# A transformer block on one Trainium2 core: six of seven down-projection pairs turned into products of 512 columns, and GELU in one activation

## The chip, the core and the metric

The kernel runs on one core of one Trainium2 chip. The metric is the device time of one execution in microseconds; where several runs are given, their median counts. The core has five engines with a queue each, which run side by side and meet at semaphores: TensorE (PE: matrix products into PSUM), VectorE (DVE), ScalarE (ACT), GpSimd (POOL) and SyncE (SP), which here issues nearly all DMAs.

## What is computed

One block on x [2048, 512]: attention with 32 query and 8 key/value heads over the last 512 cached keys, then a gated feed-forward layer with 1792 inner columns. Shifts, scales and gates come from a conditioning vector.

```python
h = _layernorm(x) * (1 + ca) + sa
x = x + ga * attention(h, k_cache, v_cache, wq, wo)
h = _layernorm(x) * (1 + cb) + sb
x = x + gb * ((gelu(h @ w_gate) * (h @ w_up)) @ w_down)     # gelu: tanh form
```

Inputs and outputs are float32.

## The kernel before

**Number format.** PE works in float16. Each float32 operand is split into a high and a low half (`halves`, `split_post`, the two lines in `result`), and one product is three matmuls, low-high, high-high and high-low (`mm3`, line 85, whose matmuls all carry line 89). Scales per weight tile keep the halves in range (`f_spread`, `d_spread`); column tables such as `fsc`, `finv`, `dsc`, `dysc` hold them and their inverses.

**Stages.** The rows are worked in two halves of 1024, each as two blocks of 512 (`qb`) of four tiles of 128. Attention is a list of 128 units (row half, head pair, block, head) in four steps each, T = 512 steps in all; its order is written out by hand, step by step, inside `tc.manual_schedule`: entries under `at(t, ...)` run at step t, and DMA loads get due times from `sched` and spare positions from `spare`. In the second half of these steps the feed-forward weights are prepared too: `prep_set` for gate and up weights and `prep_wd` for down weights load them, scale and split them on POOL, and store the halves in HBM (`store`), from where `fetch` brings them back later.

**The feed-forward stage** comes after the hand-ordered part. There only the SP queue keeps the written order; for the other engines a planner puts the instructions in order at build time, by priority (the order in which the program lists them) and by when its model says that inputs and buffers are ready. On the chip each queue then runs in that fixed order. The inner dimension has 14 tiles, taken as 7 pairs (NP); per row half and pair n there is a set of products for gate (m = 0) and one for up (m = 1), so q counts 28 of them (NQ), q = 2n + m. Each set is a 2 x 2 block product by seven block products instead of eight (a Strassen-Winograd form): `PROD` names their operands, `CHAIN` the PSUM bank (a, b or c) into which each is accumulated, `ORDER` = (1, 2, 6, 7, 5, 4, 3) their order. Bank a is read by ACT between products 1, 6, 7 and 4 of its chain (`keep`), and the next product of the chain must wait for that copy. One block product is two groups of three matmuls with 512 columns. `result` takes each finished block "11", "21", "12" or "22" (inner tile, row block): for gate it applies GELU in four instructions (ACT square, DVE, ACT tanh, DVE), for up it multiplies the two and splits the outcome into the halves `at`, A[n, key].

**Down-projection.** `y_tasks` makes for one row tile of 128 and one pair two times three matmuls: the `at` slice is the stationary operand, the prepared weights (`wo`, fetched from `kept`) are the moving one with 512 output columns. The result lies with rows on partitions, and DVE adds it, scaled by a column `dysc`, to the running row tile `acc` (line 942). That is 8 tasks of 6 matmuls a pair and row half. The loop at the end of `block_kernel` puts such tasks (`nexty`) between the products: at positions 1, 2, 5 and 6 of the seven, `y_next` takes one. `tick` counts positions for things put off by `put_off`. When the last pair of a row half is added, `f_final` stores the row tile to the output and later loads the next half's tile `y1` (attention's result, stored to HBM by `attn_final`) into the freed buffer. There are 8 `acc` buffers.

**Turning by DMA** is in the kernel already: the softmax rows `p` and the normalised rows of the second half (`ln_turned`, `xh` to `xt`) are turned by `dma_start_transpose` on two-byte elements, issued by SP.

**PSUM.** Eight banks: 5 under the tag "acc" (also for b and c of the sets and for `py`), 2 under "s", 1 under "qa".

Of the kernel before, what the change touches and what calls it, by code (L numbers as in the profile page):

```python
# [9 lines left out]

F32 = mybir.dt.float32
F16 = mybir.dt.float16
BF16 = mybir.dt.bfloat16
AF = mybir.ActivationFunctionType
ALU = mybir.AluOpType
AX = mybir.AxisListType

P = 128
# [20 lines left out]
GU = 2.0 ** -38  # L39
PRE = 2.0 ** -20  # L40
TINY = 1e-36
NOT = 10
LDGAP = 1
NRAW = 5
NRW = 2
GW = 3
NACC = 5
NP16 = 4
# [7 lines left out]
SETPOS = (20, 14, 13, 12, 10, 8)  # L56
SETPOS2 = (18, 12, 11, 10, 9, 7)
TAIL = 12
GELU_A = 0.044715
GELU_C = 0.7978845608028654  # L60


@with_exitstack
def block_kernel(ctx: ExitStack, tc: tile.TileContext, x, kT, v, wq, wo, wg, wu, wd, cT, wc, wm, out):
# [105 lines left out]
        ST[name] = const.tile([P, n], F32, name=name)  # L170

    for name, n in (("kmax", HKV), ("kinv", HKV), ("vmax", HKV), ("vsc", HKV), ("wsc", HQ // 2), ("qsc", HQ // 2),
                    ("ksc", HQ // 2), ("osc", HKV), ("ysc", HKV), ("fsc", NF), ("finv", NF), ("tsc", NF),
                    ("dsc", NF // 2), ("dysc", NF // 2), ("ma", 1), ("mf", 1), ("gam", 2)):
        stats(name, n)

    def col(name, i=0):
        return ST[name][:, i:i + 1]
# [99 lines left out]
    def o_spread(qd, m, more):  # L278
# [10 lines left out]

        then(second)  # L290

    def f_spread(i, m):
        w = little("lw", 1, 2)
        norm2(w, m, 2, 1.0 / TOP13)
        pool_ts(col("finv", i), w, col("mf"))
        pool_ts(col("tsc", i), col("finv", i), GELU_A * GELU_C)
        then(lambda: nc.vector.reciprocal(col("fsc", i), w))

    def d_spread(n, m, more):
        w, t = little("lw", 1, 2), little("lt", 1, 2)  # L300
        norm2(w, m, 2, 1.0)
        pool_ts(w, w, col("gam", 1), 1.0 / TOP14)
        pool_ts(w, w, 1e-30, 1.0, ALU.max)
        pool_ts(t, col("finv", 2 * n), 2.0 ** 19, col("finv", 2 * n + 1))
        pool_ts(col("dysc", n), t, 2.0 ** 19, w)

        def second():
            nc.vector.reciprocal(col("dsc", n), w)
            more()

        then(second)
# [636 lines left out]
    def attn_final(ti):  # L948
        y1[ti] = dram.tile([P, D], F32, name=f"y{ti}")
        dma(y1[ti], acc[ti])  # L950
        nxt = (ti + 2 * QT) % NT
        if ti < 2 * QT:
            own, steps = ln_tile(2, ti, lambda: acc[ti])
            own()
            for d, fn in zip((1, 5, 8, 9, 10, 12, 13), steps):
                at(("w", now[0] + d), fn)
            at(now[0] + 12, lambda: load_acc(nxt, rows_of(x, nxt)))
        else:
            ln_last(ti - 2 * QT)
            at(now[0] + 3, lambda: load_acc(nxt, y1[nxt]))  # L960

    def scores(t):
        u, i = divmod(t, 4)
# [291 lines left out]
    def f_items(q, hold=None):  # L1255
        n, m = divmod(q, 2)
        st = {}
        done = set()

        def add(k, src):  # L1260
            nc.vector.tensor_tensor(st[k], st[k], st[src], op=ALU.add)

        def gelu(key, src):
            b = {}

            def square():
                b["sq"] = pool.tile([P, QB], F32, tag="k", name="sq", bufs=2)
                nc.scalar.activation(b["sq"], src, AF.Square, scale=col("finv", f_scale(q)))

            def inner():  # L1270
                nc.vector.scalar_tensor_tensor(b["sq"], b["sq"], 1.0 / GELU_A, src, op0=ALU.add, op1=ALU.mult)

            def tanh():
                nc.scalar.activation(b["sq"], b["sq"], AF.Tanh, scale=col("tsc", f_scale(q)))

            def outer():
                dst = tmp("fg") if key == "21" else src
                nc.vector.scalar_tensor_tensor(dst, b["sq"], 1.0, src, op0=ALU.add, op1=ALU.mult)
                G[n, key] = dst

            return square, inner, tanh, outer

        def result(key, src):
            if m == 0:
                for step in gelu(key, src):
                    step()
            else:
                g = G.pop((n, key))
                nc.vector.scalar_tensor_tensor(g, g, 0.5 * GU, src, op0=ALU.mult, op1=ALU.mult)  # L1289
                t = pair("ot", "at", NOT)  # L1290
                nc.scalar.activation(t[:, 0, :], g, AF.Copy)  # L1291
                nc.vector.tensor_tensor(t[:, 1, :], g, t[:, 0, :], op=ALU.subtract)
                A[n, key] = t

        def out_(key, src):
            if not hold:
                result(key, src)
            else:
                hold.append(gelu(key, src))

        def place(k):
            if m == 0:
                return tmp("fg")
# [72 lines left out]

    def prep_wd(n, b):
        m, st = {}, {}
        outs = [staged() for _ in range(2)]

        def load(k):
            st[k] = raw("raw")
            dma(st[k], wd[(2 * n + k) * P:(2 * n + k + 1) * P, :])

        def stat(k):
            if not m:
                m["m"] = little("lm", 4, dtype=BF16)
            sumsq(m["m"][:, k:k + 1], st[k])

        def more():  # L1390
            m["g"] = pool.tile([P, D], F32, tag="gs", name="gs", bufs=1)
            pool_ts(m["g"], rows[5], col("dsc", n))
# [8 lines left out]
        sched(b, (lambda: load(0), [lambda: stat(0), nop]), b + 7)  # L1401
        sched(b + 1, (lambda: load(1), [lambda: stat(1), spread, nop]), b + 4, b + 9)
        for k in range(2):
            sched(b + 7 + 2 * k, (outs[k][1], [lambda k=k: make(k), lambda k=k: store(("wd", n, k), outs[k][0]["t"], 0)]), b + 10 + 2 * k)

    at(T // 2 + 34, lambda: mod_row(5))
    for n in range(NP):
# [1 line left out]
        prep_set(2 * n, b)  # L1409
        prep_set(2 * n + 1, b + 13)  # L1410
        prep_wd(n, b + 21)
    for k in range(2):
        at(T - 1 + 2 * k, lambda k=k: WO.update({("f", 0, k): fetch(("wd", 0, k), get_wo())}))
# [4 lines left out]
    pending = {"raw": [], "rw": []}  # L1418
    loads.sort(key=lambda l: l[0])
    released = {"raw": [0] * NRAW, "rw": [0] * NRW}  # L1420
    for pos, (load, steps), kind, ahead in loads:
        assert len(pos) == len(steps), (pos, len(steps))
        go = pos[0] - ahead
# [140 lines left out]
        at(("f", q, k), *fns)  # L1564

    for n in range(1, 2 * NP):
        for k in range(2):
            f_at(2 * n + 1, 2 * k, lambda n=n, k=k: WO.update({("f", n, k): fetch(("wd", n % NP, k), get_wo())}))
    for q in range(3, NQ):
        for k, at_ in ((0, 2), (3, 2), (1, 3), (2, 4)):  # L1570
            f_at(q - 1, at_, lambda q=q, k=k: set_fetch(("f", q), ("f", q % (2 * NP)), k))
# [18 lines left out]
                step(q + 2 * off, fn)  # L1590

    def f_final(ti):
        if ti >= 2 * QT:
            dma(rows_of(out, ti), acc[ti])
        else:
            put_off(2, lambda: dma(rows_of(out, ti), acc[ti]))
            put_off(5, lambda: load_acc(ti + 2 * QT, y1[ti + 2 * QT]))

    f_done = {(0, k) for k in ORDER} | {(1, 1), (1, 2), (1, 6)}
    for q in range(NQ):  # L1600
        n, m = divmod(q, 2)
        its = items(NG + q) if q < 2 else f_items(q)
        for k, pk in enumerate(ORDER):
            if (q, pk) not in f_done:
                all_of(its[pk])
            run(("f", q, k))
            tick()
            if k in ((1, 2, 5, 6) if q < NQ - 1 else (1, 5)):
                y_next()
        if m == 1:  # L1610
            for qi, (a, b) in enumerate((("11", "21"), ("12", "22"))):
                for i in range(QT):
                    nexty.append(y_tasks((2 * (n // NP) + qi) * QT + i, [lambda n=n, a=a: A[n, a], lambda n=n, b=b: A[n, b]],
                                         [("f", n, 0), ("f", n, 1)], col("dysc", n % NP), f_final if n % NP == NP - 1 else None))
    while nexty:
        y_next()
    while waits_:
        tick()
    assert not later, list(later)
# [34 lines left out]
```

## Time and profile before

| | |
|---|---|
| three timed runs | 1749.55, 1749.55, 1749.95 us; median 1749.55 |
| span of the profiled execution | 1746.6 us, its own time; the median of the runs is 2.95 us more |
| matmuls of the down-projection | 672 |
| clock granted to PE | full in every slice |

The profile is one execution. The span runs from the first to the last instruction; what lies around it (the 2.95 us) is not in the trace. Busy time of an engine counts its instructions, without waits. In a group row the engine, the operation, the tile written and the tiles read stand first, then the shapes, the count, busy us and mean ns; behind the second bar stands the idle time of the engine ahead of these instructions and what ended it. Timeline rows begin with the start and the length in us.

### The profile page before, as it was taken

The numbers are of one execution on the slowest core, as the hardware profiler recorded it, in microseconds if no ns is written. First come the engines' busy times: TensorE is split into PE (matmuls) and PEld (weight loads), VectorE is DVE, ScalarE is ACT, GpSimd is POOL, SyncE is SP. The second block draws the span as 40 slices with busy tenths as digits, with TensorE's granted clock in tenths as the row PEclk, the third lists the DMA queues.
The fourth block names the chain that finished last, engine by engine and source line by source line (L and its number), as shares of the span: only waits on it lengthen the run. The fifth ranks groups of instructions, "written<-read, shape, count | busy, mean of one in ns | idle before, by whom it ended". The sixth has DMA issues, their size and how long they took to land.

```text
span 1746.6 us, 25966 instructions
## 1 busy us (share of the span) xinstructions
PE 1724.3 (99%) x8080; PEld 792.8 (45%) x8082; DVE 1449.5 (83%) x2509; ACT 1248.3 (71%) x2806; POOL 906.2 (52%) x1127
## 2 busy tenths in 40 slices
PE   7999999999999999999999999999999999999999
PEld 5444444444444444444444444444444444444443
DVE  7898898888889999888888888888886788667676
ACT  6988788888879777888777777878774555334342
POOL 4889778776788884655474565555521224000000
PEclk9999999999999999999999999999999999999999
DMA  7999999999999998999999999999985763252222
GB/s 235 219 206 212 209 217 206 223 208 221 212 218 232 207 211 182 212 211 234 208 197 218 203 219 202 210 214 216 193 181 137 207 185 99 83 178 87 88 76 76
DMA packets 667499, 329.72 MB, mean 189 GB/s; under 512 B 561504, under 2 KB 580192, under 8 KB 667360
## 3 DMA queue, kind: packets, MB, share of 16 engines
q1 hardware_dynamic: 667072, 327.54, 81.9%
q8 instruction: 64, 1.05, 0.3%
q14 instruction: 75, 0.61, 0.1%
q10 hardware_dynamic: 288, 0.52, 0.1%
HBM read 131.73 MB, written 59.90 MB: 110 GB/s over the span
## 4 chain that ended last, share of the span: by engine, by line
PE 85%; DVE 4%; ACT 4%; issue 3%; DMA 2%; POOL 1%; SPq 0%; POOLq 0%; ACTq 0%; DVEq 0%
PE py L89 24%; PE ps L89 17%; PE po L89 17%; PE qa L89 8%; PE fa L89 6%; PE qc L89 4%; PE fc L89 3%; PE qb L89 2%; PE fb L89 1%; ACT ee L982 1%; PE pq L89 1%; ACT p L994 1%; DVE nm L973 1%; DMA cb<-hs 1%; POOL xh L534 1%
## 5 line engine op out<-in xcount | busy, mean ns | idle before, releaser
L982 ACT ACTIVATE ee<-ps,nm 128x512 f32<-128x512 f32 x512 | 350.2, 684 | 199.7 <-DVE nm L973 196.4
L999 DVE SCALAR_TENSOR_TENSOR p<-ee,rr,p 128x512 f16<-128x512 f32 x512 | 458.6, 896 | 4.1 <-ACT p L994 3.6
L973 DVE TENSOR_REDUCE nm<-ps 128x1 f32<-128x512 f32 x512 | 350.4, 684 | 113.0 <-PE ps L89 109.9
L89 PE MATMUL ps<-k,qt 128*128 128x512 f16 x1536 | 414.9, 379 | 5.4 <-ACT ee L982 4.4
L89 PE MATMUL po<-pt,v 128*128 128x512 f16 x1536 | 373.0, 379 | 1.6 <-DMA pt<-p 1.6
L994 ACT ACTIVATE p<-ee,rr 128x512 f16<-128x512 f32 x512 | 364.4, 712 | 12.4 <-DVE rr L990 9.0
L89 PE MATMUL py<-wo,ot 128*128 128x512 f16 x1536 | 371.5, 379 | 0.0
L89 PEld LDWEIGHTS <-w 128*128 128x128 f16 x2184 | 213.5, 98 | 259.8 <-issue 2.0
L89 PEld LDWEIGHTS <-v 128*128 128x128 f16 x1536 | 149.9, 98 | 183.7 <-DMA pt<-p 2.3
L89 PEld LDWEIGHTS <-ot 128*128 128x128 f16 x1536 | 150.2, 98 | 181.7 <-DVE ot L730 0.5
L89 PEld LDWEIGHTS <-qt 128*128 128x128 f16 x1536 | 145.9, 98 | 176.6 <-issue 4.0
L89 PE MATMUL py<-wo,at 128*128 128x512 f16 x672 | 161.6, 379 | 0.3 <-ACT at L1291 0.3
L730 DVE SCALAR_TENSOR_TENSOR ot<-po,ot 128x512 f16<-128x512 f32 x128 | 87.8, 686 | 30.0 <-ACT ot L729 29.3
L89 PEld LDWEIGHTS <-at 128*128 128x128 f16 x672 | 65.6, 98 | 80.0 <-ACT at L1291 0.7
L942 DVE SCALAR_TENSOR_TENSOR acc<-py,dysc,acc 128x512 f32<-128x512 f32 x112 | 81.2, 746 | 23.4 <-PE py L89 20.6
L982 ACT ACTIVATION_READ_ACCUMULATOR ee<-ps,nm 128x1 f32 x512 | 99.9, 195 | 0.0
L942 DVE SCALAR_TENSOR_TENSOR acc<-py,ysc,acc 128x512 f32<-128x512 f32 x128 | 94.7, 740 | 3.6 <-PE py L89 3.6
L89 PE MATMUL qa<-t,w 128*128 128x512 f16 x348 | 84.9, 379 | 0.0
L89 PE MATMUL fa<-t,w 128*128 128x512 f16 x336 | 82.0, 379 | 0.9 <-ACT fg L875 0.9
L729 ACT ACTIVATE ot<-po 128x512 f16<-128x512 f32 x128 | 73.8, 577 | 4.7 <-PE po L89 4.7
L234 POOL TENSOR_TENSOR lw<-lw,half__86 128x1 f32<-128x1 f32 x37 | 21.5, 582 | 105.8 <-DVE lw L184 105.8
L1291 ACT ACTIVATE at<-fg 128x512 f16<-128x512 f32 x56 | 35.0, 625 | 55.8 <-DVE fg L1289 55.7
(225 smaller groups left out, 2505.4 us busy)
## 6 DMA issues: line engine op xcount, KB each, us to landing
w<-kept SPq DMA_DIRECT2D x123, 256.0 KB, 3.2
wo<-kept SPq DMA_DIRECT2D x60, 256.0 KB, 3.7
raw<-in_wo SPq DMA_DIRECT2D x56, 256.0 KB, 3.2
kept<-stage SPq DMA_DIRECT2D x56, 256.0 KB, 3.3
kept<-w SPq DMA_DIRECT2D x39, 256.0 KB, 3.4
rw<-in_wq SPq DMA_DIRECT2D x38, 256.0 KB, 3.2
hs<-hf SPq DMA_DIRECT2D x32, 256.0 KB, 2.9
pt<-p SPq DMA_TRANSPOSE x512, 3.5
```

The lines of the kernel that those rows point to most:

```text
L89: nc.tensor.matmul(ps, a, b, start=first and n == 0, stop=last and n == 2, skip_group_check=chain)
L234: nc.gpsimd.tensor_tensor(out, out, half_, op=ALU.pow)
L534: nc.gpsimd.tensor_tensor(t[:, 1, :], st["x"], t[:, 0, :], op=ALU.subtract)
L729: nc.scalar.activation(t[:, 0, :], src, AF.Copy, scale=scale)
L730: return lambda: nc.vector.scalar_tensor_tensor(t[:, 1, :], src, scale, t[:, 0, :], op0=ALU.mult, op1=ALU.subtract)
L942: nc.vector.scalar_tensor_tensor(acc[ti], st["p"], by, acc[ti], op0=ALU.mult, op1=ALU.add)
L973: nc.vector.tensor_reduce(nm, E[t]["ps"], axis=AX.X, op=ALU.max, negate=True)
L982: nc.scalar.activation(e, E[t]["ps"], AF.Exp, bias=E[t]["nm"], scale=1.0, accum_out=sm[:, t % 2:t % 2 + 1])
L994: nc.scalar.activation(p16[:, 0, :], E[t]["e"], AF.Copy, scale=E[t]["r"])
L999: nc.vector.scalar_tensor_tensor(p16[:, 1, :], E[t]["e"], E[t]["r"], p16[:, 0, :], op0=ALU.mult, op1=ALU.subtract)
L1291: nc.scalar.activation(t[:, 0, :], g, AF.Copy)
```

## The change

Six of the seven pairs of each row half (`turned(n)`: all but the last) make the down-projection in turned form: the weights are the stationary operand and the activations the moving one, so the result has output columns on partitions and 512 rows along a bank. As both sides are 2 x 2 blocks, the same seven-product form is used: `prep_wd` now also prepares the four combined weight blocks (3.5 pieces of 256 KB instead of 2), `sums_of` the four combined activation blocks (each a POOL subtraction, an ACT copy for the high half and a POOL subtraction for the low one). `yt_tasks` makes 14 tasks of three matmuls a pair (seven products for each of two column halves p), one after each product of the sets; each is followed by `yt_add` on DVE into one of eight sums `yt`, which stay in the `acc` buffers for six pairs. The gate weights of the block (`rows[5]`) move into a column table `dyc`. After the sixth pair `yt_turn` splits each sum into its two half-words (ACT), turns it with a DMA transpose, and loads the rows `y1` into the freed buffers; `yt_rows` puts the half-words together again (ACT) and adds them to `acc` (POOL). The seventh pair goes by `y_tasks` as before, and `f_final` acts on a tile's second call. GELU becomes one ACT instruction, `Gelu_apprx_tanh`; a factor that the old form carried moves into a column `gsc`. Buffers: `NOT` 10 to 12, a ring of its own for the raw down weights, a smaller DMA scratch.

```diff
-NOT = 10
+NOT = 12
...
+    def turned(n):
+        return n % NP < NP - 1
...
         def gelu(key, src):
-            b = {}
-            def square():
-                nc.scalar.activation(b["sq"], src, AF.Square, scale=col("finv", f_scale(q)))
-            def inner():
-                nc.vector.scalar_tensor_tensor(b["sq"], b["sq"], 1.0 / GELU_A, src, op0=ALU.add, op1=ALU.mult)
-            def tanh():
-                nc.scalar.activation(b["sq"], b["sq"], AF.Tanh, scale=col("tsc", f_scale(q)))
-            def outer():
+            def apply():
                 dst = tmp("fg") if key == "21" else src
-                nc.vector.scalar_tensor_tensor(dst, b["sq"], 1.0, src, op0=ALU.add, op1=ALU.mult)
+                nc.scalar.activation(dst, src, AF.Gelu_apprx_tanh, scale=col("finv", f_scale(q)))
...
+                nc.vector.scalar_tensor_tensor(g, g, col("gsc", n % NP), src, op0=ALU.mult, op1=ALU.mult)
+                if not turned(n):
+                    parts(key, G.pop((n, key)), nc.vector)
+                elif key != "12":
+                    parts(key, g, nc.vector)
+                else:
+                    sums_of()
+        def parts(key, g, eng):
+            t = A[n, key] = pair("ot", "at", NOT)
+            nc.scalar.activation(t[:, 0, :], g, AF.Copy)
+            eng.tensor_tensor(t[:, 1, :], g, t[:, 0, :], op=ALU.subtract)
+        def sums_of():
+            g = {k: G.pop((n, k)) for k in ("11", "12", "21", "22")}
+            for o, a, b in (("11", "12", "11"), ("12", "22", "12"), ("22", "22", "11"), ("21", "21", "22")):
+                nc.gpsimd.tensor_tensor(g[o], g[a], g[b], op=ALU.subtract)
+                parts({"11": "t1", "12": "t3", "22": "t2", "21": "t4"}[o], g[o], nc.gpsimd)
...
+    def yt_add(n, c, qb, ps):
+        by = ST["dyc"][:, KT * (n % NP) + c:KT * (n % NP) + c + 1]
+        key = (n // NP, c, qb)
+        if key in YT:
+            nc.vector.scalar_tensor_tensor(YT[key], ps, by, YT[key], op0=ALU.mult, op1=ALU.add)
+        else:
+            YT[key] = pool.tile([P, QB], F32, tag="acc", name="yt", bufs=2 * QT)
+            nc.vector.tensor_scalar(YT[key], ps, by, None, op0=ALU.mult)
+    def yt_turn(g, c, qb):
+        def split():
+            u = YR["u", c, qb] = pool.tile([P, 2, QB], U16, tag="p16", name="yu", bufs=NP16)
+            nc.scalar.activation(u.rearrange("p h r -> p r h"), YT[g, c, qb].bitcast(U16).rearrange("p (r h) -> p r h", h=2), AF.Copy)
+        def turn():
...
+            nc.sync.dma_start_transpose(YR["t", qb][:, c], YR.pop(("u", c, qb)).rearrange("p a b -> p (a b)"))
+        split()
+        put_off(2, turn)
...
+                put_off(3, lambda ti=ti: load_acc(ti, y1[ti]) or back.add(ti))
+    def yt_rows(g, qb):
...
+            nc.scalar.activation(r.bitcast(U16).rearrange("p (c q h) -> p c q h", c=KT, h=2), t[:, :, :, :, i], AF.Copy)
+            nc.gpsimd.tensor_tensor(acc[ti], acc[ti], r, op=ALU.add)
+            f_final(ti)
+    YORDER = (1, 2, 6, 5, 7, 3, 4)
...
+            tasks += [[(lambda k=k, f=group: f(k), lambda k=k, f=post: f(k))] for k in YORDER]
...
+            if n and k == 2 and m == 0 and turned(n - 1):
+                nexty += yt_tasks(n - 1)
-            if k in ((1, 2, 5, 6) if q < NQ - 1 else (1, 5)):
+            if k in ((1, 2, 5, 6) if q < NQ - 1 else (1, 5)) or (n and turned(n - 1)):
                 y_next()
+            if (q, k) in ((NQ - 2, 3), (NQ - 2, 5)):
+                y_next()
-        if m == 1:
+        if m == 1 and not turned(n):
```

More of the change, by code (lines that the diff above doesn't have):

```diff
@@ L295, in f_spread @@
         pool_ts(col("finv", i), w, col("mf"))
-        pool_ts(col("tsc", i), col("finv", i), GELU_A * GELU_C)
         then(lambda: nc.vector.reciprocal(col("fsc", i), w))
+        if i % 2 == 0:
+            g = col("gsc", i // 2)
+            pool_ts(g, col("finv", i), 1.0 / GU)
+            then(lambda: nc.vector.reciprocal(g, g))
     def d_spread(n, m, more):
@@ L301, in d_spread @@
         norm2(w, m, 2, 1.0)
-        pool_ts(w, w, col("gam", 1), 1.0 / TOP14)
+        pool_ts(w, w, 1.0 if turned(n) else col("gam", 1), 1.0 / TOP14)
         pool_ts(w, w, 1e-30, 1.0, ALU.max)
@@ L305, in d_spread @@
         pool_ts(col("dysc", n), t, 2.0 ** 19, w)
+        if turned(n):
+            pool_ts(ST["dyc"][:, KT * n:KT * (n + 1)], cols[:, 5, :], col("dysc", n))
         def second():
@@ L1390, in more @@
         def more():
-            m["g"] = pool.tile([P, D], F32, tag="gs", name="gs", bufs=1)
-            pool_ts(m["g"], rows[5], col("dsc", n))
+            if not turned(n):
+                m["g"] = pool.tile([P, D], F32, tag="gs", name="gs", bufs=1)
+                pool_ts(m["g"], rows[5], col("dsc", n))
         def spread():
@@ L1399, in make, with out, keep_it, tt @@
             halves(outs[k][0]["t"], st[k])
[L1401 to L1404, printed above, removed]
+        def out(k):
+            return outs[k][0]["t"] if k < 3 else outs[k][0]["t"][:, :, l]
+        def keep_it(k):
+            return lambda: store(("wd", n, k), out(k), 0)
+        def tt(o, a, c, op):
+            nc.gpsimd.tensor_tensor(o, a, c, op=op)
+        def d0():
+            times(st[0], col("dsc", n))
+            times(st[1], col("dsc", n))
+            halves(out(0)[:, :, l], st[0][:, l])
+            halves(out(0)[:, :, r], st[1][:, l])
+        def d1():
+            halves(out(3), st[1][:, r])
+            tt(st[1][:, r], st[0][:, r], st[1][:, r], ALU.add)
+            tt(st[0][:, r], st[0][:, l], st[0][:, r], ALU.subtract)
+        def d2():
+            tt(st[0][:, l], st[1][:, r], st[0][:, l], ALU.subtract)
+            tt(st[1][:, l], st[1][:, l], st[0][:, l], ALU.subtract)
+        if not turned(n):
+            sched(b, (lambda: load(0), [lambda: stat(0), nop]), b + 7, kind="wr")
+            sched(b + 1, (lambda: load(1), [lambda: stat(1), spread, nop]), b + 4, b + 9, kind="wr")
+            for k in range(2):
+                sched(b + 7 + 2 * k, (outs[k][1], [lambda k=k: make(k), keep_it(k)]), b + 10 + 2 * k)
+            return
+        sched(b, (lambda: load(0), [lambda: stat(0), nop]), b + 10, kind="wr")
+        sched(b + 1, (lambda: load(1), [lambda: stat(1), spread, d2, nop]), b + 4, b + 9, b + 11, kind="wr")
+        sched(b + 7, (outs[0][1], [d0, keep_it(0)]), b + 10)
+        sched(b + 8, (outs[3][1], [d1, keep_it(3)]), b + 11)
+        sched(b + 10, (outs[1][1], [lambda: halves(out(1), st[0]), keep_it(1)]), b + 13)
+        sched(b + 11, (outs[2][1], [lambda: halves(out(2), st[1]), keep_it(2)]), b + 14)
     at(T // 2 + 34, lambda: mod_row(5))
@@ L1566, in block_kernel @@
     for n in range(1, 2 * NP):
-        for k in range(2):
-            f_at(2 * n + 1, 2 * k, lambda n=n, k=k: WO.update({("f", n, k): fetch(("wd", n % NP, k), get_wo())}))
+        for k, at_ in ((0, 1), (2, 3), (1, 4), (3, 5)) if turned(n) else ((0, 1), (1, 4)):
+            f_at(2 * n + 1, at_, lambda n=n, k=k: wd_fetch(n, k))
     for q in range(3, NQ):
@@ L1592, in f_final @@
     def f_final(ti):
+        assert ti in back
+        if ti not in halfway:
+            return halfway.add(ti)
         if ti >= 2 * QT:
@@ new lines, in yt_rows @@
+    def yt_rows(g, qb):
+        t = YR.pop(("t", qb)).rearrange("p c (h i) q -> p c q h i", h=2)
+        for i in range(QT):
+            ti = 2 * QT * g + QT * qb + i
+            assert ti in back
+            r = raw("yr")
+            nc.scalar.activation(r.bitcast(U16).rearrange("p (c q h) -> p c q h", c=KT, h=2), t[:, :, :, :, i], AF.Copy)
+            nc.gpsimd.tensor_tensor(acc[ti], acc[ti], r, op=ALU.add)
+            f_final(ti)
+    ADDS = {1: ((0, 0),), 2: ((0, 0),), 6: ((0, 1),), 5: ((1, 1),), 7: ((1, 1),), 4: ((1, 0),), 3: ((0, 1),)}
@@ new lines, in block_kernel, with yt_tasks, group, post @@
+    YORDER = (1, 2, 6, 5, 7, 3, 4)
+    LAST = {2: (0, 0), 7: (1, 1), 3: (0, 1), 4: (1, 0)}
+    def yt_tasks(n):
+        tasks = []
+        for p in range(2):
+            st = {}
+            bk = banks(st, {"a": ("acc", "ya", NACC) if p else ("qa", "ya", 1), "b": ("acc", "yb", NACC), "c": ("acc", "yc", NACC)})
+            def group(k, p=p, bk=bk):
+                a, b = PROD[k]
+                x, start = CHAIN[k]
+                ci, off = YCOL[a]
+                w, t = WO["f", n, ci], A[n, {"b11": "11", "b21": "21", "b22": "22"}.get(b, b)]
+                sl = slice(off + p * P, off + (p + 1) * P)
+                mm3(bk(x)(), w[:, 0, sl], w[:, 1, sl], t[:, 0, :], t[:, 1, :], start, k in (2, 4, 3), True)
+            def post(k, p=p, st=st):
+                (i, qb), = ADDS[k]
+                yt_add(n, 2 * i + p, qb, st[CHAIN[k][0]])
+                if n % NP == NP - 2 and k in LAST:
+                    i, qb = LAST[k]
+                    c, g = 2 * i + p, n // NP
+                    put_off(1, lambda: yt_turn(g, c, qb))
+                    if p and k in (3, 4):
+                        put_off(7 if g else 9, lambda: yt_rows(g, qb))
+            tasks += [[(lambda k=k, f=group: f(k), lambda k=k, f=post: f(k))] for k in YORDER]
+        return tasks
```

53 lines of the change are left out of this document (29 added, 24 removed).

## The prediction

> **What bounds the kernel now.** I read the head of the page first: whose time is the span?
>
> ```profile
> span 1746.6 us, 25966 instructions
> PE 1724.3 (99%) x8080; PEld 792.8 (45%) x8082; DVE 1449.5 (83%) x2509; ACT 1248.3 (71%) x2806; POOL 906.2 (52%) x1127
> ```
>
> TensorE (PE) is busy for all but 22 us. Since a busy share can hide slow matmuls, the stages come next, as stretches: most of the second attention half, where down-projection weights are prepared, then the feed-forward stage in two stretches. Columns: length; then busy us and instruction count of PE, PEld, DVE, ACT, POOL; granted clock; DMA share; GB/s.
>
> ```profile
> 700.00:1300.00 600.00, 598.49 (x2806) 273.24 (x2805) 507.01 (x882) 480.98 (x1130) 326.98 (x397) 1.00 0.97 210
> 1343.00:1500.00 157.00, 156.10 (x723) 70.50 (x722) 125.37 (x185) 78.86 (x127) 46.91 (x51) 1.00 0.52 155
> 1500.00:1700.00 200.00, 200.00 (x928) 90.62 (x927) 137.03 (x210) 79.95 (x126) 0.00 (x0) 1.00 0.33 104
> ```
>
> From 1500 to 1700 us PE is never idle and the clock is whole, so a matmul of 512 columns costs 200/928 = 0.2155 us there; a removed one is worth that if nothing takes its place. DVE has 31% free, ACT 60%, POOL everything, DMA two thirds. In attention the DMA engines are at 0.97, so what the change adds there matters. Last, the waits of PE in the feed-forward stage up to the last pair:
>
> ```profile
> PE fa L89 <- ACT u L875: 0.4, 1, 0.4
> PE fa L89 <- DVE fg L1278: 0.3, 1, 0.3
> PE fa L89 <- ACT fg L875: 0.2, 1, 0.2
> ```
>
> 0.9 us in 391: the order fixed at build time lets PE wait for almost nothing. PE's stream is the bound, and the end hangs on what follows its last matmul.
>
> **Matmuls removed.**
>
> ```profile
> L89 PE MATMUL py<-wo,at 128*128 128x512 f16 x672 | 161.6, 379 | 0.3 <-ACT at L1291 0.3
> ```
>
> 672 are 14 pairs of 48 (8 row tiles, two f tiles, three terms). A turned pair takes 7 products x 2 column halves x 3 terms = 42. With 12 turned pairs (6 of 7, for two row halves) 72 go: 72 x 0.2155 = **-15.5 us**.
>
> **Vector work of a turned pair.** Group rows of the stage (mean ns is the second number behind the bar):
>
> ```profile
> L942 DVE SCALAR_TENSOR_TENSOR acc<-py,dysc,acc 128x512 f32<-128x512 f32 x97 | 70.7, 746 | 22.8 <-PE py L89 20.1 <-DMA wo<-kept 2.5
> L1292 DVE TENSOR_TENSOR at<-fg,at 128x512 f16<-128x512 f32 x48 | 34.9, 728 | 10.8 <-ACT at L1291 9.7
> L1274 ACT ACTIVATE sq<-sq,tsc 128x512 f32<-128x512 f32 x47 | 33.9, 721 | 32.0 <-DVE sq L1271 32.0
> L1291 ACT ACTIVATE at<-fg 128x512 f16<-128x512 f32 x48 | 30.0, 626 | 49.1 <-DVE fg L1289 49.0
> L1271 DVE SCALAR_TENSOR_TENSOR sq<-sq,fg 128x512 f32<-128x512 f32 x35 | 26.2, 748 | 2.7 <-ACT sq L1268 2.6
> L1289 DVE SCALAR_TENSOR_TENSOR fg<-fg,u 128x512 f32<-128x512 f32 x24 | 17.3, 721 | 0.3
> L1261 DVE TENSOR_TENSOR u<-u,fc 128x512 f32<-128x512 f32 x24 | 16.4, 683 | 9.7 <-ACT u L875 7.2 <-PE fc L89 2.5
> L564 POOL TENSOR_TENSOR cb<-cb 128x512 f32<-128x512 f32 x8 | 11.8, 1479 | 0.2
> ```
>
> DVE loses two GELU steps on four blocks (8 x 0.75) and one low part (0.73), and gains six sums (14 `yt_add` against 8 row sums, 6 x 0.746): -2.3 us a pair. ACT loses four activations (4 x 0.72) and gains three copies (3 x 0.63): -1.0. POOL gains four differences and four low parts: 8 x 1.48 = 11.8 us against a pair's time of (84 + 42) x 0.2155 = 27.2 us. All of it fits beside PE. No row shows the new activation's price; as 512 columns from SBUF it has the neighbours' 0.72 us, and at double that ACT still has room.
>
> What can cost PE is lateness. Behind the last gate-times-up block come its sum and product on DVE (0.68 + 0.72, some 0.2 for each of two hand-offs, an estimate: 1.8 us), then POOL's eight steps. Operand t2 is whole after six or seven, so 1.8 + 6 x 1.27 (the short POOL time, quoted with the tail below) = 9.4 us at best, 1.8 + 7 x 1.48 = 12.2 us at worst. Its product stands in slot 4 of the next gate set: five set products (5 x 6 matmuls) and four down products of 3 before it are 42 x 0.2155 = 9.1 us. So it is 0.3 to 3.1 us late; PE hides that if its queue has the next set product ahead, and loses it if not. Between 0 and 12 x 3.1 = 37 us, I take **+2.0 us**, 0.17 a pair, since the nearest rows, the three waits above, show the same build-time order covering chains of ACT and DVE nearly whole. A shorter filler between set products 6 and 7 (3 matmuls where 6 stood) falls under the same term. The SP queue gets 16 transposes waiting for their ACT copies, with weight fetches behind them; these lead by several products.
>
> A rule of the Trainium skill speaks against the POOL steps: SBUF — State Buffer, section "SBUF: two separate sides", says that a DVE instruction with two SBUF inputs and a GpSimd one that reads SBUF share a port pair, and that one blocks the other for a whole instruction. The gap from 1.27 to 1.48 us between POOL rows agrees with some blocking, not with a whole step each time. By the rule taken strictly, seven such DVE steps a pair would each wait out a POOL step, 7 x 1.27 = 8.9 us, an estimate that takes DVE from 17.2 to 26.1 of 27.2 us (0.685 x 28.4 = 19.5 now, less 2.3): no bound of its own, but it would put t2 at the late end, and the sum 29 us higher. Part of the second rival's chance is for it.
>
> **Attention stage.**
>
> ```profile
> kept<-stage SPq DMA_DIRECT2D x56, 256.0 KB, 3.3
> ```
>
> Preparing a turned pair's weights stores 3.5 pieces instead of 2: 6 x 1.5 x 256 KB = 2.4 MB, at 210 GB/s 11 us of the DMA engines' time, against 0.03 x 600 = 18 us free. POOL gets about four more full steps a pair, 6 x 4 x 1.48 = 36 us where 273 are idle. No matmul there reads these. Bounds 0 and 11; I take **+0.5 us**. The eight loads of `y` that leave the end of attention are off PE's path and count nothing; were the weight fetches that follow late, the same 0.5 covers it.
>
> **The tail.** Timeline rows: PE's last two groups, the last DVE sum, and a POOL step and an SP transpose issue without company; then ACT copies of 256 and 512 columns and two landing times.
>
> ```profile
> 1733.03 1.46 PE L89 MATMUL fc<-b,w 128*128 128x512 f16 x6
> 1734.74 8.05 PE L89 MATMUL py<-wo,at 128*128 128x512 f16 x36 [0.25 <-ACT at L1291]
> 1742.83 0.75 DVE L942 SCALAR_TENSOR_TENSOR acc<-py,dysc,acc 128x512 f32<-128x512 f32 x1 [0.55 <-PE py L89]
> 1456.89 1.27 POOL L564 TENSOR_TENSOR cb<-cb 128x512 f32<-128x512 f32 x1
> 1407.21 1.23 SPq L539 DMA_TRANSPOSE xt<-xh  x1
> ...
> L510 ACT ACTIVATE b<-hf 128x256 f16<-128x256 f32 x24 | 9.1, 417 | 0.0
> L533 ACT ACTIVATE xh<-xs 128x512 f16<-128x512 f32 x8 | 4.9, 620 | 0.1
> ...
> acc<-y SPq DMA_DIRECT2D x16, 256.0 KB, 3.2
> xt<-xh SPq DMA_TRANSPOSE x8, 4.2
> ```
>
> Before, PE ends at 1742.8 and the span 3.8 us later: one sum, one store (3.0 us from the last sum's end). After it, call E the end of the last set product (1734.5 before). Behind E stand a last turned product and eight row tasks, 3 + 48 matmuls = 11.0 us. The turned product is done at E+0.65, its sum (0.75) at E+1.8, its split by ACT at E+3.5: 1024 half-words at 0.62 + 2 x (0.62 - 0.42) = 1.0 us by the two ACT rows, and some queueing. The transpose lands 4.2 us later, E+7.7. SP issues four loads of `y` behind it, landing from about E+8 on. Eight rows then need an ACT copy (1.0) and a POOL add (1.27) each. POOL is the slower, and its first add also needs the fifth row task's sum, E + 0.65 + 5 x 1.29 + 0.95 = E+8.1. So POOL ends at E + 8.2 + 8 x 1.27 = E+18.4, and the last store at E+21.4. That is 10.4 us behind PE's end against 3.8: **+6.6 us**. Below it 0, if the eight adds were done while PE still works; above it about 9, with POOL at 1.48 us and another 1 us of landing.
>
> **Sum.** 1746.6 - 15.5 + 2.0 + 0.5 + 6.6 = 1740.2 us span. The runs' median of 1749.55 us is 2.95 above the profiled span, which I carry over: **1743.2 us**. A difference of 0.2%, 3.5 us, is about what a measurement of this kernel can tell from no change.
>
> **Rivals.**
> - The tail is hidden, as DVE and ACT are then idle and the transposes may land early: 1743.2 - 6.6 = 1736.6 us. Against it: eight POOL adds in a row behind a sum that PE makes late. Chance 0.13.
> - The sums are late (it ends slower): PE's queue, fixed at build time, has the t2 product ahead of what is ready, and PE stands still once a pair, with everything behind it in its queue. Without the 2.0 for it the sum is 1741.2; each microsecond of lateness adds 12. At 0.7 us a pair the gain is gone; at the middle, 1.7 us, it is 1761.6 us, at 3.1 us 1778. For it: eight POOL steps in a row with ACT between them, longer beside DVE. Against it: the three waits, and two set products that PE can take first. Chance 0.15.
> - Attention's DMA engines, at 0.97, take the 2.4 MB badly and transposes of `p` land late: +5 to +11, so 1748 to 1754 us. For it the share; against it PE's whole stretches at that share. Chance 0.08.
> - The new activation doesn't sit with the copies around it, so tables change back and forth:
>
> ```profile
> L121 ACT ACT_TABLE_LOAD x1 | 1.3, 1283 | 1.7 <-PEq L1646 1.7
> ```
>
> Before, one load serves all. If each of 56 GELUs took two, 112 x 1.28 = 144 us would go onto ACT, in front of the copies that free PE's banks; even a fifth of it on PE gives 1772 us. Chance 0.04. ScalarE: Activation LUTs, section "Table sets: the hidden batching unit", has copy and identity in every set and gelu in a set other than exp's, which would make it one more load in all, 1.3 us beside PE; the single load here for exp, tanh, square and copy agrees as far as it goes.
>
> **How the numbers follow.** The forecast has the remaining 0.60; its own range is 1738 to 1748, from the tail's bounds and up to 6 us of lateness. Below 1746.05 us (faster) lie 0.54 of it and the hidden tail, 0.67. Within 0.2%: 0.06 of it, 0.04 of the DMA case, 0.03 of slight lateness, 0.13. Slower: 0.12 lateness, 0.04 DMA, 0.04 tables, 0.20. The range 1736 to 1754 leaves out the worse lateness (0.10), the tables (0.04) and about 0.03 below.
>
> **What would show it.** 600 matmuls of down-projection instead of 672, and PE's stretches from 1500 on still whole. Right: PE ends near 1730 and the page's chain ends in POOL adds behind PE's end, by some 10 us. Wrong: waits of PE for POOL or ACT of a microsecond, a dozen times (lateness); waits for `pt` before 1300 (DMA); more than two table loads; or the last POOL add within 2 us of PE's last matmul (hidden tail).

## The result, and the profile after

The changed kernel takes 1795.15 us (median of 4 runs) against 1749.72: ratio 1.0259, interval 1.0247 to 1.0271. It is slower by 45 us where 6.5 us less were forecast; the time lies far outside the range.

The page's head of the changed kernel, with the slices of PE and of its granted clock:

```profile
span 1793.8 us, 26201 instructions
PE 1721.3 (96%) x8008; PEld 788.1 (44%) x8010; DVE 1424.1 (79%) x2464; ACT 1318.9 (74%) x2819; POOL 1070.1 (60%) x1292
PE   7999999999999999999999999999999999699974
PEclk9999999999999999999999999999999999899997
```

The 72 matmuls are gone (8080 to 8008). PE is as full as before except in two places, slice 35 and the last two, where it goes idle; the granted clock drops in slice 35 and in the last. The waits of the feed-forward stage (from 1300 us on) name what it waits for:

```profile
PE fa L89 <- ACT u L884: 15.2, 2, 8.3
PE fa L89 <- ACT fg L884: 13.8, 4, 7.6
PE fa L89 <- ACT fu L884: 8.1, 1, 8.1
PE ya L89 <- ACT at L1296: 3.2, 2, 2.8
PE py L89 <- ACT at L1296: 3.1, 1, 3.1
```

That is 43.4 us of PE behind ACT, in ten waits, against 1.6 us before. POOL isn't in the list. L884 is the copy that frees bank a between products of a set (line 875 before). What does ACT do meanwhile? Its new groups, and those of POOL and the GELU, in the same stage:

```profile
L1664 ACT ACTIVATE yu<-yt 128x1024 uint16<-128x1024 uint16 x16 | 74.1, 4878 | 5.8 <-DVE yt L1655 5.7
L1275 ACT ACTIVATE fg<-fg,finv 128x512 f32<-128x512 f32 x39 | 28.1, 719 | 31.9 <-DVE fg L1269 31.8
L1685 ACT ACTIVATE yr<-yv 128x1024 uint16<-128x1024 uint16 x16 | 17.6, 1159 | 0.0
...
L1302 POOL TENSOR_TENSOR fg<-fg 128x512 f32<-128x512 f32 x48 | 62.4, 1300 | 139.8 <-DVE fg L1286 138.7
L1297 POOL TENSOR_TENSOR at<-fg,at 128x512 f16<-128x512 f32 x48 | 57.9, 1216 | 5.1 <-ACT at L1296 3.5 <-PE ya L89 1.6
```

The split of a sum into half-words takes 4.88 us; I had set 1.0. The copy back, of the same size and type, takes 1.16. The timeline at the first place shows the price:

```profile
1535.59 13.77 ACT L1664 ACTIVATE yu<-yt 128x1024 uint16<-128x1024 uint16 x3
...
1541.89 0.81 PE L89 MATMUL py<-wo,at 128*128 128x512 f16 x3
...
1549.67 0.58 ACT L884 ACTIVATE fg<-fa 128x512 f32<-128x512 f32 x1
...
1550.31 2.72 PE L89 MATMUL fa<-t,w 128*128 128x512 f16 x6 [7.60 <-ACT fg L884]
```

Three splits stand in a row in ACT's fixed queue, 13.77 us together. Behind them waits a 0.6 us copy that PE needs; PE finds work until 1542.7 and then stands for 7.6 us. The next six matmuls take 2.72 us instead of 1.46; the clock granted from 1550 to 1560 us is 0.81. Stretches (columns as in the prediction) show where this happens, and that the part between is whole:

```profile
1500.00:1550.00 50.00, 37.86 (x169) 16.45 (x167) 22.89 (x35) 39.27 (x27) 9.62 (x8) 0.94 0.39 98
1600.00:1650.00 50.00, 50.00 (x233) 22.70 (x232) 35.44 (x52) 19.06 (x31) 19.36 (x16) 1.00 0.33 106
1700.00:1750.00 50.00, 35.77 (x158) 15.53 (x157) 23.95 (x36) 29.50 (x22) 9.54 (x8) 0.92 0.24 65
1750.00:1794.00 44.00, 20.34 (x66) 7.52 (x65) 12.73 (x17) 28.94 (x18) 10.33 (x8) 0.73 0.47 131
```

Both places are the turning back of a row half.

### The profile page after: what moved, and what is told of

It is laid out like the page before. It is cut to its first block, busy times and chain, and to the rows that moved or that the text cites. A ratio compares the mean times of both kernels' runs of the same rounds, so it can differ in the third digit from the quotient of the medians.

```text
span 1793.8 us, 26201 instructions
## 1 busy us (share of the span) xinstructions
PE 1721.3 (96%) x8008; PEld 788.1 (44%) x8010; DVE 1424.1 (79%) x2464; ACT 1318.9 (74%) x2819; POOL 1070.1 (60%) x1292
## 5 line engine op out<-in xcount | busy, mean ns | idle before, releaser
L1302 POOL TENSOR_TENSOR fg<-fg 128x512 f32<-128x512 f32 x48 | 62.4, 1300 | 139.8 <-DVE fg L1286 138.7
L89 PE MATMUL fa<-t,w 128*128 128x512 f16 x336 | 87.7, 396 | 25.6 <-ACT fg L884 10.6
L1296 ACT ACTIVATE at<-fg 128x512 f16<-128x512 f32 x92 | 58.0, 638 | 64.5 <-DVE fg L1286 38.4
L89 PE MATMUL ya<-at,wo 128*128 128x512 f16 x288 | 77.5, 379 | 4.5 <-ACT at L1296 3.2
L396 POOL TENSOR_TENSOR rs<-rs,nhalf 128x1 f32<-128x1 f32 x32 | 18.7, 584 | 102.8 <-DVE rs L390 99.9
L1664 ACT ACTIVATE yu<-yt 128x1024 uint16<-128x1024 uint16 x16 | 74.1, 4878 | 5.8 <-DVE yt L1655 5.7
```

The lines of the kernel that those rows point to most:

```text
L89: nc.tensor.matmul(ps, a, b, start=first and n == 0, stop=last and n == 2, skip_group_check=chain)
L396: nc.gpsimd.tensor_tensor(st["rs"], st["rs"], nhalf, op=ALU.pow)
L1302: nc.gpsimd.tensor_tensor(g[o], g[a], g[b], op=ALU.subtract)
L1664: nc.scalar.activation(u.rearrange("p h r -> p r h"), YT[g, c, qb].bitcast(U16).rearrange("p (r h) -> p r h", h=2), AF.Copy)
```

## The experiments

The theory: the split is slow because of the way it writes, and its 16 instructions block ACT's queue. The rival was the one of the prediction, late combined operands. Each ratio is to runs of the kernel before on the same chip (medians 1750.15 to 1750.27 us).

**The split walked the other way round.**

```diff
-            nc.scalar.activation(u.rearrange("p h r -> p r h"), YT[g, c, qb].bitcast(U16).rearrange("p (r h) -> p r h", h=2), AF.Copy)
+            nc.scalar.activation(u, YT[g, c, qb].bitcast(U16).rearrange("p (r h) -> p h r", h=2), AF.Copy)
```

> The same split of the sums into half-words, walked in the other order: it reads every second half-word (4 bytes apart) and writes one row of 512 after the other, where the changed kernel reads in order and writes by turns into two rows 1 KB apart. Theory (the 16 split copies are slow because of the way they write, and block the ACT queue in front of the copies that free PE's banks): a split takes about 1.1 us instead of 4.88, as the copies back do, PE's waits for ACT fall from some 39 us to under 5, the clock stays whole, and the time is 1743 us (1738 to 1748) by the terms of the prediction. Rival (the combined operands are late, as forecast as the slower case): the split has no part in it, the time stays above 1780. Second rival (splits are slow for reading or for the 16-bit integer type): a split stays at 4 to 5 us and the time near 1795.

1755.48 us, ratio 1.0028 (1.0018 to 1.0038). Both kernels run the same instructions in the same order on ACT, DVE and POOL, and on PE throughout the feed-forward stage, so nothing but the split itself differs. So 39.7 of the 45 us were the order of the split's writes. The split's row, then PE's waits from 1700 us on and the end of the timeline:

```profile
L1664 ACT ACTIVATE yu<-yt x16: 1040/1052/1057, 1510.0 to 1727.0; 128x1024 uint16<-128x1024 uint16 x16
...
PE py L89 <- ACT at L1296: 5.8, 2, 5.5
PE fa L89 <- ACT u L884: 2.0, 1, 2.0
...
1733.90 5.42 ACT L1685 ACTIVATE yr<-yv 128x1024 uint16<-128x1024 uint16 x5 [2.31 <-DMA yv<-yu]
1738.65 10.38 POOL L1686 TENSOR_TENSOR acc<-acc,yr 128x512 f32<-128x512 f32 x8 [25.57 <-DMA acc<-y]
1739.90 7.88 PE L89 MATMUL py<-wo,at 128*128 128x512 f16 x24 [5.49 <-ACT at L1296]
1747.83 5.00 SPq L95 DMA_DIRECT2D out_y<-acc  x8
```

The split is at 1.05 us, yet the kernel is 12 us above the forecast. At the end ACT waits 2.3 us for a transpose and then makes five copies back, while the high half of the last block stands behind them in its queue. PE waits 5.5 us for that half and runs its last 24 matmuls in 7.88 us instead of 5.2 (granted clock 0.68 from 1740 to 1748 us). The eight stores come bunched, since SP keeps its order: the first goes out behind the seventh of the eight adds.

**GELU alone**, on the kernel before:

```diff
-            b = {}
...
+            def apply():
                 dst = tmp("fg") if key == "21" else src
-                nc.vector.scalar_tensor_tensor(dst, b["sq"], 1.0, src, op0=ALU.add, op1=ALU.mult)
+                nc.scalar.activation(dst, src, AF.Gelu_apprx_tanh, scale=col("finv", f_scale(q)))
                 G[n, key] = dst
...
-            return square, inner, tanh, outer
+            return (apply,)
```

> The kernel before with GELU as one activation and nothing else of the change. Theory: ACT and DVE have room in the feed-forward stage, so 112 DVE and 168 ACT steps less change the time by under 2 us: 1748 to 1750. Rival (tables change back and forth between the new activation and the copies): dozens of table loads, over 1770. Second rival (the planner uses the shorter chains): faster by 2 to 4 us.

1747.55 us, ratio 0.9985 (0.9977 to 0.9994): a gain of 2.6 us, just outside the theory's range and inside the second rival's 2 to 4 us. There is one more table load and no going back and forth, so the rival on tables is refuted.

**Ways of writing**, by copies of 1024 elements behind the end of the kernel before. The lines are, in order: ACT writing by turns into two rows; POOL by turns; ACT by turns in float16; DVE by turns; ACT by turns with four-byte elements; ACT reading in order and writing every second half-word of one row, in two passes (the expectation has it reading by turns, which the edit doesn't do); ACT writing every second half-word, in one pass; ACT reading by turns and writing in order; ACT plain; POOL and DVE reading by turns and writing in order.

```diff
+        nc.scalar.activation(zd, s16, AF.Copy)
+        nc.scalar.activation(zd.rearrange("p (h r) -> p r h", h=2), s16.rearrange("p (r h) -> p r h", h=2), AF.Copy)
+        nc.scalar.activation(zd.rearrange("p (h r) -> p h r", h=2), s16.rearrange("p (r h) -> p h r", h=2), AF.Copy)
...
+        nc.scalar.activation(z2.rearrange("p (r h) -> p r h", h=2)[:, :, 0], s16, AF.Copy)
...
+        nc.vector.tensor_copy(zd.rearrange("p (h r) -> p r h", h=2), s16.rearrange("p (r h) -> p r h", h=2))
...
```

> The kernel before, with copies of 1024 elements added behind its end, each three times, on zeroes: ACT plain; ACT reading in order and writing by turns into two rows 1 KB apart (the split of the changed kernel); ACT the other way round; the same in float16; ACT writing to every second half-word of one row; ACT by turns with four-byte elements 2 KB apart; ACT reading by turns and writing every second; then the two orders on DVE and on POOL. Theory (it is the write by turns of single half-words): only the writes by turns of 2-byte elements take 4 to 5 us on ACT, whatever the type, all others 1.0 to 1.2. Rival (any 2-byte write that is not contiguous is slow): the write to every second half-word is slow too. Second rival (the integer type is slow): the plain integer copy is slow and float16 by turns is not. Third rival (far jumps in general): four-byte elements by turns are as slow. The time itself tells nothing here.

```profile
L1634 ACT ACTIVATE zd<-zs 128x1024 uint16<-128x1024 uint16 x3 | 14.4, 4806 | 0.1
L1642 POOL COPY zd<-zs 128x1024 uint16<-128x1024 uint16 x3 | 14.1, 4697 | 326.7 <-DVE zd L1641 326.7
L1636 ACT ACTIVATE zd<-zs 128x1024 f16<-128x1024 f16 x3 | 14.1, 4689 | 0.0
L1640 DVE COPY zd<-zs 128x1024 uint16<-128x1024 uint16 x3 | 8.3, 2753 | 53.0 <-ACT zd L1639 53.0
L1638 ACT ACTIVATE zd<-zs 128x1024 f32<-128x1024 f32 x3 | 6.3, 2088 | 0.0
L1639 ACT ACTIVATE zd<-zs 128x1024 uint16<-128x1024 uint16 x3 | 4.3, 1435 | 0.1
L1637 ACT ACTIVATE zd<-zs 128x1024 uint16<-128x1024 uint16 x3 | 4.0, 1334 | 0.0
L1635 ACT ACTIVATE zd<-zs 128x1024 uint16<-128x1024 uint16 x3 | 3.5, 1151 | 0.1
L1633 ACT ACTIVATE zd<-zs 128x1024 uint16<-128x1024 uint16 x3 | 3.2, 1056 | 20.7 <-POOL zd L1643 13.7 <-DVE zs L1623 7.0
L1643 POOL COPY zd<-zs 128x1024 uint16<-128x1024 uint16 x3 | 3.1, 1039 | 0.2
L1641 DVE COPY zd<-zs 128x1024 uint16<-128x1024 uint16 x3 | 2.1, 694 | 0.1
```

It is the writing: read by turns and written in order costs 1.15 us, written by turns 4.81. The type plays no part (float16 4.69). All three engines show it, at 4.0 to 4.6 times their time in order. A step of four bytes within a row costs little (1.33 and 1.44 against 1.06). Here the theory was too narrow: four-byte elements by turns are slow too, at 2.09 us, beside 1.06 for the plain two-byte copy (no plain four-byte copy was run). They differ in size and in distance (2 KB), so which of the two halves the price stays open.

**Slow splits in one row half only.**

```diff
...
+            v = YT[g, c, qb].bitcast(U16)
+            if g:
+                nc.scalar.activation(u, v.rearrange("p (r h) -> p h r", h=2), AF.Copy)
+            else:
+                nc.scalar.activation(u.rearrange("p h r -> p r h"), v.rearrange("p (r h) -> p r h", h=2), AF.Copy)
```

> The changed kernel with the slow split for the first row half only (8 of 16 splits at 4.88 us), the second row half's swapped. Theory (each slow split blocks ACT, and PE loses what the cover there does not hide): PE's waits for ACT near 1500 to 1570 us come back as in the changed kernel, some 14 us, with a few us at a lower clock; none beyond what the swapped split has at the end; 1755.5 + 14 to 18 = 1770 to 1774. Rival (the loss is at the end of the chain alone): within 3 us of 1755.5.

1771.91 us (two runs), ratio 1.0122 (1.0104 to 1.0141): 16.4 us above the swapped split, as expected. PE's wait between 1335 and 1710 us is back where the slow ones are:

```profile
L1668 ACT ACTIVATE yu<-yt x8: 4752/4886/5037, 1508.1 to 1555.0; 128x1024 uint16<-128x1024 uint16 x8
L1666 ACT ACTIVATE yu<-yt x8: 1041/1045/1057, 1721.2 to 1740.7; 128x1024 uint16<-128x1024 uint16 x8
...
PE fa L89 <- ACT fg L884: 14.1, 4, 7.8
```

The other eight then cost 23 us (1795.15 - 1771.91). That they cost more because the end has less other work for PE is likely, but wasn't tested.

**The rest, 12 us: copies back on DVE.** From here on every run has the swapped split; the edits shown come on top of it.

```diff
...
+            to = r.bitcast(U16).rearrange("p (c q h) -> p c q h", c=KT, h=2)
+            if g:
+                nc.vector.tensor_copy(to, t[:, :, :, :, i])
+            else:
+                nc.scalar.activation(to, t[:, :, :, :, i], AF.Copy)
+            (nc.vector if g and i % 2 else nc.gpsimd).tensor_tensor(acc[ti], acc[ti], r, op=ALU.add)
```

> The swapped split, and for the second row half the eight copies back (1.16 us each on ACT) on DVE, and every second of the eight adds on DVE instead of POOL. Theory (what is left of the loss lies at the end: the copies back stand in ACT's queue in front of the last block's high half, PE waits 5.5 us for it and then starts at a reduced clock, and eight POOL adds close the chain): PE's wait for that block falls under 1.5 us, the span ends about 5 us behind PE's last matmul instead of 8.4, and the time falls from 1755.5 to 1743 to 1747. Rival (what is left comes from stalls in the middle, by late combined operands): within 2 us of 1755.5.

1755.96 us, ratio 1.0031 (1.0020 to 1.0043): no gain, against the theory as I had put it, and just where the rival, stalls in the middle, had it. PE's wait for the last block fell only by half, and the span now ends 10.7 us behind PE instead of 8.4:

```profile
PE py L89 <- ACT at L1296: 3.0, 2, 2.7
...
1732.14 1.30 DVE L1687 COPY yr<-yv 128x1024 uint16<-128x1024 uint16 x2 [1.74 <-DMA yv<-yu]
1733.35 0.75 DVE L1286 SCALAR_TENSOR_TENSOR fg<-fg,gsc,u 128x512 f32<-128x512 f32 x1
```

The copies now stand in DVE's queue, behind the transpose, in front of the product of that same block (L1286). The wait for the transpose moved with them. So this run shows that moving these copies and half of the adds to DVE brings nothing; it doesn't tell the tail from the middle. The next run does.

**Five of seven pairs turned.**

```diff
-        return n % NP < NP - 1
+        return n % NP < NP - 2
...
-                if n % NP == NP - 2 and k in LAST:
+                if n % NP == NP - 3 and k in LAST:
```

(`y_tasks` then calls `f_final` for the last pair only.)

> The swapped split, with five of seven pairs turned instead of six, so that the turning back of the second row half comes a whole pair earlier, beside the last sets of products, and two pairs go by row tasks. 12 matmuls more than with six: 2.6 us. Theory (the loss is the tail): PE's end and the span's end stand as before the change (about 4 us apart), no wait over 1.5 us behind the last set; 1742 to 1746. Rival (stalls in the middle by late operands): the two untaken pairs bring back 2 x 0.5 us and cost 2.6; 1754 to 1757. A third: the copies back now hold up ACT in front of the copies of the last sets, and the loss only moves; 1748 to 1752.

1746.26 us, ratio 0.9982 (0.9973 to 0.9991), 0.3 us above the theory's range and far below the rival's: 9.2 us less than with six, with 12 matmuls more. The copies back and the adds now run while PE works, and PE ends 4.0 us ahead of the span's 1744.1:

```profile
1717.22 5.43 ACT L1685 ACTIVATE yr<-yv 128x1024 uint16<-128x1024 uint16 x5 [3.25 <-DMA yv<-yu]
1718.89 10.31 POOL L1686 TENSOR_TENSOR acc<-acc,yr 128x512 f32<-128x512 f32 x8 [34.32 <-DMA acc<-y]
...
1731.50 8.57 PE L89 MATMUL py<-wo,at 128*128 128x512 f16 x36 [0.21 <-ACT at L1296]
```

**Both together**, five of seven and the edit for DVE:

> Both: five of seven pairs turned, and for the second row half the copies back on DVE with half of the adds. Theory (tail): as with five of seven alone or 1 to 2 us better, 1741 to 1745, since with a pair of time in hand ACT and POOL hide the copies anyway. If ACT's queue is what holds PE there, clearly better than five of seven alone, by 3 us or more.

1751.93 us, ratio 1.0011 (1.0002 to 1.0019): 5.7 us worse than five of seven alone. From 1690 us on PE's waits for DVE sum to 4.2 us, against 1.3 with five of seven alone. DVE is the wrong place for these copies and adds; the expectation missed that.

**Low parts of the combined operands on DVE**, with six of seven:

```diff
-                parts({"11": "t1", "12": "t3", "22": "t2", "21": "t4"}[o], g[o], nc.gpsimd)
+                parts({"11": "t1", "12": "t3", "22": "t2", "21": "t4"}[o], g[o], nc.vector)
```

> The swapped split, with the four low parts of the combined operands of each pair on DVE (0.73 us each) instead of POOL (1.22), so that POOL's chain is four steps instead of eight and t2 and t4 are whole some 4 us earlier. Theory (late combined operands cost little, 5 us in all at most): 1752 to 1757, as with the swapped split alone. Rival (lateness of POOL's chain is what keeps the saving of the middle small): PE's waits between 1343 and 1700 us vanish and the time falls to 1747 to 1751. If DVE becomes the bound of a pair: over 1758.

1751.65 us, ratio 1.0007 (0.9998 to 1.0016): 3.8 us less than the swapped split, between the theory's range and the rival's. From the end of the first set to the end of the 26th (last `fc` matmul of each, by the timelines) it takes 361.4 us, against 366.8 with the swapped split and 377.3 before. Not all of these 5.4 us are late operands. This edit makes the planner order all engines anew, and the stretch holds 12 matmuls fewer (1659 against 1671), 2.6 us that come behind it. PE's waits in it fall from 4.8 to 2.4 us; the longest that goes is one of 1.7 us for a weight fetch, and only one of the six waits, 0.8 us, names a combined operand (`ya` for `at`). So POOL's chain costs some 4 us by the runs, but through which wait isn't shown. At the end a single wait of 6.5 us for the last block's high half stays.

**Five of seven and low parts on DVE**, and the same with only t2 and t4 there:

> The swapped split, five of seven pairs turned, and the low parts of the combined operands on DVE. Theory (two separate losses: the tail, taken by five of seven, and POOL's eight-step chain, taken by the low parts on DVE): both gains add, 1746.3 less about 4, 1741 to 1744, faster than the kernel before by 6 to 9 us. Rival (both take the same loss): 1746 to 1748. If DVE, with the row tasks of one more pair, is too full: over 1748.

> As before it, with only the low parts of t2 and t4, the last two of POOL's chain, on DVE. If it is the chain's end that matters (t2 and t4 are wanted in the slots that come soonest after them), the gain is the same, 1741 to 1744; if it is POOL's load as a whole, or its port, half of it, 1744 to 1745.

1741.27 us, ratio 0.9948 (0.9936 to 0.9961), and 1743.43 us, ratio 0.9960 (0.9947 to 0.9974). The gains add, as expected: the first is 9.0 us faster than the kernel before. Its PE, too, ends 4.0 us ahead of the span. Two low parts on DVE bring 2.8 of the 5.0 us: the time lies in the range set for the chain's end, the share nearer to half, which stood for POOL's load as a whole. The two intervals overlap and the planned orders differ, so this stays open.

```profile
span 1739.5 us, 26119 instructions
...
1727.17 8.34 PE L89 MATMUL py<-wo,at 128*128 128x512 f16 x36 [0.21 <-ACT at L1296]
```

## Why the prediction was wrong, step by step

**The step that failed: the split's price.** I put the split at 1.0 us, from ACT rows of 256 and 512 elements that all write in order. None of these rows wrote by turns, so I should have bounded it from both sides; I gave a single estimate and asked only about its place in the tail. It takes 4.88 us, sixteen times. The first eight I hadn't costed at all: I named the SP queue's wait for them, but not what is queued behind them on ACT. That queue holds the copies that free PE's banks. This is 39.7 us, shown by the swapped split and by slow splits in one row half only.

**Matmuls removed:** right. 600 of the down-projection are left, and from 1600 to 1700 us PE is never idle:

```profile
L89 PE MATMUL ya<-at,wo 128*128 128x512 f16 x288 | 77.5, 379 | 4.5 <-ACT at L1296 3.2 <-DMA w<-kept 0.6 <-DVE yt L1655 0.6
L89 PE MATMUL yc<-at,wo 128*128 128x512 f16 x144 | 40.7, 379 | 0.0
L89 PE MATMUL py<-wo,at 128*128 128x512 f16 x96 | 25.2, 412 | 3.1 <-ACT at L1296 3.1
L89 PE MATMUL yb<-at,wo 128*128 128x512 f16 x72 | 21.7, 379 | 0.0
```

**Lateness of the combined operands:** 2.0 us was too little. The low parts on DVE are worth 3.8 us alone and 5.0 with five of seven. That PE loses this by waiting for the operands, as the term has it, isn't shown: the edit changed the order of the instructions as well. The rival, PE standing still once a pair, was wrong: with the swapped split there are six waits in the whole middle, 4.8 us in all. The kernel came out slower, as in that rival, but not by it.

**Port sharing:** the rule of the Trainium skill (SBUF — State Buffer, "SBUF: two separate sides") would have let a DVE step with two SBUF inputs wait out a whole POOL step of 1.27 us. In the changed kernel single steps agree (min/median/max in ns):

```profile
L1286 DVE SCALAR_TENSOR_TENSOR fg<-fg,gsc,u x28: 734/742/1571, 1359.6 to 1774.4; 128x512 f32<-128x512 f32 x28
L1286 DVE SCALAR_TENSOR_TENSOR fg<-fg,gsc,fu x14: 740/752/1727, 1335.4 to 1745.3; 128x512 f32<-128x512 f32 x14
L1286 DVE SCALAR_TENSOR_TENSOR fg<-fg,gsc,fa x14: 731/744/748, 1363.3 to 1771.5; 128x512 f32<-128x512 f32 x14
```

Here `u` and `fu` lie in SBUF and `fa` in PSUM. Nine of the first 42 take over 0.9 us, each with a POOL step under way; none of the last 14 does. Before it was 5 of 42 already. With the low parts on DVE (6 of 44, against 4 of 56) that is about one meeting a pair, where the strict reading had seven. (A median step went from 0.69 to 0.74 us; as it takes 0.75 with GELU alone, that comes with the factor `gsc`, not with POOL.) The prediction's sum for that reading is off as well: at the late end, 12 x 3.1 us in place of 2.0 makes 35 us more, not 29; 29 us is how far the 1778 us lies above the kernel before.

**Tail:** the 6.6 us counted only what comes behind PE's end. With the swapped split the span ends 8.4 us behind PE, against 3.8 before, so 4.6 us there; but ahead of that PE itself stands 5.5 us for a block that waits behind copies that wait for a transpose, and its last 24 matmuls take 2.7 us longer. I had let the copies back queue for one another, not the last block behind them, nor the stores bunch on SP: the last POOL add ends at 1749.0, and the span 7.2 us later where I had 3.0.

**Attention:** not resolved. The first set ends at 1330.7 us after against 1329.5 before, but at 1331.0 with GELU alone, which leaves the stage's transfers as they were, and at 1333.9 with the swapped split, which leaves them as after: the executions scatter by more than the 0.5 us. PE's waits for `pt` before 1300 us sum to 1.2 us, against 1.6 before; that rival is refuted.

**Tables:** ScalarE: Activation LUTs, section "Table sets: the hidden batching unit", of the Trainium skill has copy in every set, and sets gelu apart from `gelu_apprx_tanh`, the function used here, without naming that one's set; the prediction took gelu's row for it. The trace shows one load more, and none for the copies between:

```profile
L121 ACT ACT_TABLE_LOAD x1 | 1.3, 1283 | 1.6 <-PEq L1774 1.6
L1275 ACT ACT_TABLE_LOAD x1 | 1.3, 1283 | 0.0
```

## What to carry to other kernels

Price a copy by how it writes: where an access pattern can be walked in two orders, let the output run in order and the input jump. When an instruction is put on an engine that is off the critical path, ask what stands behind it in that engine's fixed queue, and what follows if it takes several times your estimate. Work that must follow the last sum belongs a stage earlier: here one pair more in the old form (2.6 us of matmuls) brought back 9.2 us.

## What the hardware showed

1024 two-byte elements written by turns into two rows 1 KB apart take 4.81 us on ACT, 4.70 on POOL and 2.75 on DVE, against 1.06, 1.04 and 0.69 in order. Reading by turns costs ACT 0.1 us at most (1.15 against 1.06, means of three). Beside a POOL step, a DVE step with two SBUF inputs took up to 1.73 us instead of 0.75; with one of them in PSUM never over 0.75. And a wait of PE is dearer than its length: after 7.6 us of standing, six matmuls took 2.72 us instead of 1.46, at a granted clock of 0.81 from 1550 to 1560 us; after 5.5 us of standing (swapped split), 24 took 7.88 instead of 5.2, at 0.68.
